# Loading w_q and w_o through ScalarE's DMA queue in a two-layer decode kernel

## The chip, the cores and the metric

The kernel runs on one core of a Trainium2 chip. The metric is device time in microseconds (us) of one execution. Before the change it is 644.1 us, the median of three runs (643.8 to 644.4).

## The reference, cut to what matters

Two identical layers, each of an attention block over cached keys and values and a SwiGLU block, for four sequences with one new token each. Both layers read the same caches and the same weights.

```python
B, Sq, D = 4, 1, 512
Hq, Hkv, Sk, Dh = 32, 8, 8192, 128

def _A_ref(x, k_cache, v_cache, wq, wo):
    q = transpose((x @ wq).reshape(B, Sq, Hq, Dh), 0, 2, 1, 3)
    k = jnp.repeat(k_cache, 4, axis=1)
    v = jnp.repeat(v_cache, 4, axis=1)
    scores = jnp.einsum("bhqd,bhkd->bhqk", q, k) * (Dh ** -0.5)
    o = jnp.einsum("bhqk,bhkd->bhqd", _softmax(scores), v)
    return transpose(o, 0, 2, 1, 3).reshape(B, Sq, Hq * Dh) @ wo

def _B_ref(x, w_gate, w_up, w_down):
    return (_silu(x @ w_gate) * (x @ w_up)) @ w_down

for layer in range(2):
    x = x + _A_ref(_layernorm(x), k_cache, v_cache, wq, wo)
    x = x + _B_ref(_layernorm(x), w_gate, w_up, w_down)
```

All tensors are bf16. The keys of one (sequence, key head) pair are 8192 x 128 elements, 2 MB (2,097,152 bytes), and its values as much. w_q is 512 x 4096 and w_o 4096 x 512, 4 MB each. Both layers together move some 273 MB from HBM to SBUF.

## The kernel before, in words

A *unit* is one (key head, sequence) pair, 32 of them in a layer, worked on in turn. For a unit the kernel loads all its keys into one of eight slots of the SBUF buffer `kv`, and all its values into another. VectorE transposes the keys in place, eight pieces of 128 x 512 (`turn`), TensorE makes the scores of each piece (`scores`), the softmax runs over ScalarE, TensorE and VectorE (`max_p`, `max_t`, `exps`, `turn_p`, `total`), and TensorE multiplies with the values (`values`). In every fourth unit the projection of a finished key head with w_o follows (`out_proj`), and the query of the next one with w_q (`qmul`). After the last unit of a layer comes the SwiGLU block (`ffn`). At the end of layer 0 the keys and values of three units stay in their slots for layer 1.

The loads. Every load of the kernel is issued by SyncE (`T.dma("sp", ...)`), in the order of the list `items`: keys and values as `work` gives them, K0 K1 V0 K2 V1 K3 V2 K4 V3 and so on, with the weights of the SwiGLU block at the end of each layer. `pump` goes through the list and issues a load as soon as its slot (`home`) is free, and stops at the first whose slot is not. K0 to K3 go to slots 0 to 3, V0 to V2 to slots 4 to 6; K4 needs slot 0 again, and V3 stands behind K4 in the list. `finished` frees a slot and calls `pump` again; a slot of keys is free when the last scores of the unit are done.

The two weights in question. w_q is kept in `wq_sb` as four tiles of 1 MB. Their four loads stand ahead of `pump`, with the load of x (4 KB) behind the first. w_o is kept in `wo_sb`, eight loads of 512 KB, in pairs put into `items` at places 3, 6, 9 and 12:

```python
for n, it in ((3, ("wo", 0)), (6, ("wo", 1)), (9, ("wo", 2)), (12, ("wo", 3))):
    items.insert(n, it)
```

`runs` views each source in HBM as rows of up to 32 KB, a multiple of 32 rows: 64 rows of 32 KB for the keys of a unit, 32 of 32 KB for a tile of w_q, 32 of 16 KB for a part of w_o. The load of a tile is written as an instruction on SyncE's queue by name (line 136 in the profile).

Who waits for them. The first `qmul` waits for the four tiles of w_q in turn (a semaphore for each). The cast in `out_proj` waits for all eight parts of w_o (one semaphore, `hold=[T.res["wo3"].w]`). In the order of VectorE's work, the transposes of K0 stand behind the first query's casts and placing, so they too come after w_q.

Instructions of TensorE, VectorE and ScalarE are first written on a tape and issued at the end of the build (`play`, `roll`), the regular units as a loop. A load that is issued with `T.dma` goes to its engine at once, ahead of whatever the tape holds. ScalarE's stream before the change starts with the load of its table of functions (line 313), and then its tape, which starts with the logarithm of the first normalization (`deviation`, behind the first block of scores).

Of the kernel before, what the change touches and what calls it, by code (L numbers as in the profile page):

```python
# [14 lines left out]
class _Rec:  # L15
    __slots__ = ("w", "r")

    def __init__(self):
        self.w = None
        self.r = {}  # L20
# [7 lines left out]

class _Sync:
    LATE = ("pe", "dve", "act")  # L30

    def __init__(self, nc, engines, prog_sems):
        self.nc = nc
# [5 lines left out]
        self.semval = {}  # L39
        self.tape = {n: [] for n in self.LATE}  # L40

# [72 lines left out]
    def op(self, engname, fn, reads=(), writes=(), sig=True, hold=()):  # L114
        left = self._open(engname, self._need(reads, writes)) + list(hold)
        if engname in self.LATE:
            name, args, kw = fn(_Call())
# [10 lines left out]
    def dma(self, engname, parts, sem, reads=(), writes=()):  # L128
        self._wait(engname, self._need(reads, writes))
        k = id(sem)  # L130
        for out_ap, in_ap in parts:
            e = self.eng[engname]
            if in_ap.shape[0] == out_ap.shape[0]:
                ins = e.dma_start(out_ap, in_ap)
            else:
                ins = e.add_instruction(mybir.InstDMACopy(  # L136
                    name=self.nc.get_next_instruction_name(), mode="Copy", queue="qSPDynamicHW",
                    ins=e.lower_ap_dma(in_ap), outs=e.lower_ap_dma(out_ap)))
            ins.then_inc(sem, 16)
            self.semval[k] = self.semval.get(k, 0) + 16  # L140
        self._record(engname, (sem, self.semval[k]), reads, writes)
# [5 lines left out]
def bass_interleave_layers__gqa_block_cached__swiglu_ffn__decode_kernel(  # L147
# [13 lines left out]
    _, G, S, Dh = A_k_cache.shape  # L161
# [3 lines left out]
    REP = Hq // G  # L165
    P = 128
    assert Dh == P and B * Hq == P and D % P == 0 and F % P == 0 and B == 4
    KT = D // P
# [15 lines left out]
    RUN = 1 << 15  # L184
# [8 lines left out]
    with ExitStack() as es:  # L193
# [27 lines left out]
        wq_sb = sb("wq_sb", [P, KT, HqDh], BF16)  # L221
# [3 lines left out]
        wo_sb = sb("wo_sb", [P, G, REP, D], BF16)  # L225
# [27 lines left out]
        n = 2 * FO * B  # L253
# [13 lines left out]
        def few(ap):  # L267
# [17 lines left out]
        sem_w = {n: [sem(f"sem_{n}{i}") for i in range(c)]  # L285
                 for n, c in (("wq", KT), ("wo", 1), ("wg", KT), ("wu", KT), ("wd", len(WD)))}
        sem_out = sem("sem_out")
        es.enter_context(nc.Block())
        T = _Sync(nc, engines, prog)
# [8 lines left out]
        for a in range(NA):  # L298
# [11 lines left out]
        T.op("dve", lambda e: e.tensor_reduce(own[:], acc[:, 0:QB].rearrange("p (a y) -> p y a", a=NA)[:, 0:NV, :],  # L310
                                              AX.X, ALU.max),
             reads=["acc"], writes=["own"])
        nc.scalar.preload_act_table_set("natural_log_exp_and_others")
        ones = onesf[:].to_broadcast([P, P])

# [22 lines left out]
        items = []  # L338
        for L in range(2):
            seq = [it for it in work(L) if it not in kept]  # L340
            for k, v in ((29, 27), (30, 28)):

                it = ("K", L, unit_order[L][k])
                seq.remove(it)
                seq.insert(seq.index(("V", L, unit_order[L][v])), it)
            items += seq + [("wg", L)] + [("wu",)] * (L == 0) + [("wd",)]
        for n, it in ((3, ("wo", 0)), (6, ("wo", 1)), (9, ("wo", 2)), (12, ("wo", 3))):
            items.insert(n, it)
        i, j = (items.index((k, 1, unit_order[1][2 * NRES + n])) for k, n in (("K", 1), ("V", 0)))
        items[i], items[j] = items[j], items[i]  # L350
        ends = [i for i, it in enumerate(items) if it[0] == "wd"]
# [17 lines left out]
                return 0 if i == NU - 1 else (7, 2, 3, 6)[i % CYCLE]  # L369
            return {NU - 3: 1, NU - 2: 4, NU - 1: 5}.get(i, (5, 0, 4, 1)[i % CYCLE])  # L370

        def runs(src):

            n = src.shape[0] * src.shape[1] * 2
            return src.rearrange("(r k) n -> r (k n)", r=32 * -(-n // (32 * RUN)))

        def load_weight(name, i=0):
            if name == "wq":
                T.dma("sp", [(wq_sb[:, i, :], runs(A_wq[i * P:(i + 1) * P, :]))], sem_w["wq"][i], writes=[f"wq{i}"])
            elif name == "wo":  # L380
                n = G // 4
                w = REP * Dh
                T.dma("sp", [(wo_sb[:, g, :, :].rearrange("p e n -> p (e n)"), runs(A_wo[g * w:(g + 1) * w, :]))
                             for g in range(i * n, (i + 1) * n)], sem_w["wo"][0], writes=[f"wo{i}"])
            elif name == "wg":
                for k in range(KT - i):
                    T.dma("sp", [(wg_sb[k], runs(B_w_gate[k * P:(k + 1) * P, :]))], sem_w["wg"][k],
                          writes=(places if k == 0 else []) + [f"wg{k}"])
            elif name == "wu":
                for k in range(KT):  # L390
                    T.dma("sp", [(wu_sb[k], runs(B_w_up[k * P:(k + 1) * P, :]))], sem_w["wu"][k], writes=[f"wu{k}"])
            else:
                for j, (a, b) in enumerate(WD):
                    T.dma("sp", [(wd_sb[:, a:b, :].rearrange("p e n -> p (e n)"), runs(B_w_down[a * P:b * P, :]))],
                          sem_w["wd"][j], writes=[f"wd{j}"])

        def pump():
            while issued[0] < len(items):
                n = issued[0]
                it = items[n]  # L400
                if it[0][0] == "w":
                    if it[0] == "wg":
                        if not {NKEEP, NKEEP + 1} <= free:
                            return
                        free.difference_update((NKEEP, NKEEP + 1))
                    load_weight(*it)
                    issued[0] += 1
                    continue

                s = home(it)  # L410
                if s not in free:
                    return
                free.remove(s)
                kind, L, u = it
                slot_of[it] = s
                g, b = unit_gb(u)
                cache = A_k_cache if kind == "K" else A_v_cache
                if it in split:
                    for i in range(len(pieces[L, u])):
                        part(it, s, i, i + 1, sem_l[i])  # L420
                elif (L, u) in pieces:
                    part(it, s, 0, len(pieces[L, u]), sem_s[s])
                else:
                    T.dma("sp", [(kv[:, s, :], runs(cache[b, g, :, :]))], sem_s[s], writes=[f"s{s}.{q}" for q in range(NB)])
                issued[0] += 1
# [126 lines left out]

        heads = {n: [] for n in T.LATE}
        blocks = []
# [352 lines left out]
        def roll(name):  # L907
# [43 lines left out]
                at = heads[name][n + CYCLE * turns]  # L951
            T.play(name, ops[at:])

        load_weight("wq", 0)
        T.dma("sp", [(xio, A_x.rearrange("b s d -> (b s) d"))], sem_x, writes=SCR)
        for i in range(1, KT):
            load_weight("wq", i)
        pump()
        xb = bank_bf(OUTB)
        for kt in range(KT):  # L960
# [4 lines left out]
        for L in range(2):  # L965
# [20 lines left out]
            for kind, _, u in todo:  # L986
# [9 lines left out]
             writes=[SCR[1]])  # L996
        T.wait_res("sp", reads=SCR)
        nc.sync.dma_start(out.rearrange("b s d -> (b s) d"), xio).then_inc(sem_out, 16)
        nc.sync.wait_ge(sem_out, 16)
        for n in T.LATE:  # L1000
            roll(n)
# [28 lines left out]
```

## Time and profile before

| | |
|---|---|
| median of three runs | 644.1 us (643.8 to 644.4) |
| the profiled execution: its own time | 644.4 us |
| its span, first to last instruction | 642.5 us |
| busy: PE, DVE, ACT, POOL | 80%, 70%, 19%, 3% |
| moved by DMA | 273.30 MB in 12215 packets, mean 425 GB/s |
| loads of keys and of values, whole | 56 and 56 of 2048 KB |
| loads of w_q, issue to landing | 4 of 1024 KB, median 8.5 us |
| loads of w_o, issue to landing | 8 of 512 KB, median 37.3 us (24.0 to 45.2) |

The profile is of one execution. PE is TensorE, PEld its weight loads, DVE VectorE, ACT ScalarE, POOL GpSimd, SP SyncE, SPq an instruction that issues a DMA. q1 is SyncE's DMA queue; q8 and q14 are queues over which the chip fetches its own instructions. Sixteen DMA engines serve all queues, and a load is spread over all sixteen. A row of the timeline has the start, the duration, the engine and line, the operation, its tiles and count, and in brackets the idle time before it with what ended it. A row of the DMA queues has the packets, their MB, and the time that they took as a share of sixteen engines' time in the stretch asked for; a packet belongs to the stretch in which it starts. A row of the stretches has, behind the stretch, its length, each engine's busy time and count, the clock granted to TensorE, the DMA share and GB/s.

### The profile page before, as it was taken

What the parts mean: (1) busy time and instruction counts of PE and PEld (TensorE: products, weight loads), DVE (VectorE), ACT (ScalarE), POOL (GpSimd) and SP (SyncE); (2) the same over time, 40 slices, a digit from 0 to 9 for tenths busy, and PEclk for the clock granted to TensorE, in tenths of its full rate; (3) what the DMA queues carried; (4) which work ended last, traced back from release to release, by engine and by line L of the source; (5) the groups of instructions that cost most, each with busy time, mean ns of one, the idle gap of its engine ahead of it and who ended that gap; (6) DMA issues with size and microseconds to landing.
All of it is one profiled execution on the core that took longest, in us unless ns stands there. A gap on an engine that the chain in (4) does not pass through costs nothing.

```text
span 642.5 us, 13057 instructions
## 1 busy us (share of the span) xinstructions
PE 514.2 (80%) x5064; PEld 332.7 (52%) x5087; DVE 450.9 (70%) x1108; ACT 122.1 (19%) x401; POOL 19.3 (3%) x73
## 2 busy tenths in 40 slices
PE   1757697887879788787888889898887769788788
PEld 1534454554546555455556655565554535555456
DVE  2646667677776867768764749987776776776783
ACT  0111211112212212212221422221221221221222
POOL 0000000000000000000000000000000000000000
PEclk9976779689896978999999989998889897987899
DMA  8999999999999999999999999999999999999996
GB/s 355 424 427 431 441 425 428 441 435 426 431 437 437 426 430 439 433 432 426 435 420 427 420 432 430 430 429 432 435 430 430 435 435 430 430 435 437 425 424 286
DMA packets 12215, 273.30 MB, mean 425 GB/s; under 512 B 2872, under 2 KB 2880, under 8 KB 3008
## 3 DMA queue, kind: packets, MB, share of 16 engines
q1 hardware_dynamic: 12192, 272.98, 99.1%
q8 instruction: 16, 0.26, 0.2%
q14 instruction: 7, 0.06, 0.0%
HBM read 272.96 MB, written 0.00 MB: 425 GB/s over the span
## 4 chain that ended last, share of the span: by engine, by line
DMA 61%; PE 22%; DVE 13%; issue 1%; SPq 1%; ACT 1%; DVEq 0%; POOL 0%; POOLq 0%
DMA kvf<-in_A_k_cache_dram 49%; PE ps L100 22%; DMA kvf<-in_A_v_cache_dram 9%; DVE kvf L118 8%; DMA kvf<-in_B_w_up_dram 3%; DVE acc L118 2%; SPq L136 1%; DVE one L118 1%; ACT pb L118 1%; DVE pT L118 1%; DVE m L118 1%; ACT acc L118 0%; POOL zq L502 0%; DVE oT L118 0%; ACT one L118 0%
## 5 line engine op out<-in xcount | busy, mean ns | idle before, releaser
L118 DVE STREAM_TRANSPOSE kvf<-kvf 128x512 f32<-128x512 f32 x488 | 322.6, 686 | 86.7 <-DMA kvf<-in_A_k_cache_dram 86.5
L100 PE MATMUL ps<-kvf,zq 128*128 128x256 bf16 x2048 | 316.7, 297 | 17.0 <-DVE kvf L118 12.6
L100 PEld LDWEIGHTS ps<-kvf,zq 128*128 128x128 bf16 x2048 | 196.9, 108 | 80.4 <-DVE kvf L118 29.6
L118 ACT ACTIVATE pb<-m 1x128 f32<-1x128 f32 x64 | 19.7, 308 | 431.6 <-DVE m L118 431.3
L100 PE MATMUL ps<-kvf,pT 128*16 128x512 bf16 x992 | 67.8, 395 | 10.4 <-DVE rl L118 6.3
L118 DVE SCALAR_TENSOR_TENSOR acc<-ps,own,acc 128x128 f32<-128x128 f32 x186 | 65.1, 350 | 5.4 <-ACT acc L118 0.7
L100 PE MATMUL ps<-identf,one 128*1 128x128 f32 x64 | 17.7, 277 | 49.1 <-DVE one L118 48.8
L100 PEld LDWEIGHTS ps<-identf,one 128*1 128x1 f32 x64 | 5.1, 79 | 77.8 <-DVE one L118 73.9
L100 PEld LDWEIGHTS ps<-kvf,pT 128*16 128x16 bf16 x992 | 19.4, 89 | 40.6 <-issue 22.3
L118 DVE TENSOR_REDUCE one<-ps 128x1 f32<-128x256 f32 x64 | 26.0, 407 | 16.9 <-PE ps L100 16.7
L118 ACT ACTIVATE pb<-ps,one,rstd 128x256 bf16<-128x256 f32 x64 | 36.1, 565 | 2.1
L502 POOL TENSOR_TENSOR zq<-scr,quad 128x64 bf16<-128x64 bf16 x62 | 18.2, 293 | 600.3 <-PE ps L100 473.4
L100 PE MATMUL ps<-head,acc 128*128 128x4 f32 x124 | 23.5, 260 | 15.6 <-DVE acc L118 15.6
L100 PEld LDWEIGHTS ps<-head,acc 128*128 128x128 f32 x124 | 21.2, 213 | 28.3 <-DVE acc L118 26.6
L100 PEld LDWEIGHTS ps<-one,pb 1*128 1x128 f32 x128 | 21.4, 208 | 26.9 <-ACT pb L118 22.6
L118 DVE RECIPROCAL rl<-ps 128x4 f32<-128x4 f32 x64 | 10.4, 162 | 34.2 <-PE ps L100 34.2
L100 PE MATMUL ps<-one,pb 1*128 1x1 f32 x128 | 26.8, 276 | 9.3 <-ACT pb L118 9.3
L118 DVE STREAM_TRANSPOSE pT<-pb 128x256 bf16<-128x256 bf16 x64 | 26.1, 408 | 4.6 <-ACT pb L118 4.5
L100 PE MATMUL ps<-wq_sb 128*128 128x512 bf16 (+1 forms) x84 | 26.2, 380 | 1.9 <-issue 1.1
L100 PE MATMUL ps<-xn,wq_sb 128*128 128x32 bf16 x284 | 19.6, 182 | 6.7 <-DMA wq_sb<-in_A_wq_dram 6.1
L100 PEld LDWEIGHTS ps<-o,wo_sb 128*128 (+1 forms) x256 | 20.0, 100 | 8.3 <-issue 4.5
L100 PE MATMUL ps<-o,wo_sb 128*128 128x32 bf16 x256 | 23.5, 181 | 0.8 <-DVE o L118 0.6
(72 smaller groups left out, 251.0 us busy)
## 6 DMA issues: line engine op xcount, KB each, us to landing
kvf<-in_A_k_cache_dram SPq DMA_DIRECT2D x56, 2048.0 KB, 28.9
kvf<-in_A_v_cache_dram SPq DMA_DIRECT2D x56, 2048.0 KB, 32.6
kvf<-in_A_k_cache_dram SPq DMA_DIRECT2D x7, 1024.0 KB, 7.7
kvf<-in_A_v_cache_dram SPq DMA_DIRECT2D x7, 1024.0 KB, 11.7
wq_sb<-in_A_wq_dram SPq DMA_DIRECT2D x4, 1024.0 KB, 8.5
wo_sb<-in_A_wo_dram SPq DMA_DIRECT2D x8, 512.0 KB, 37.3
kvf<-in_B_w_gate_dram SPq DMA_DIRECT2D x7, 448.0 KB, 18.0
kvf<-in_B_w_down_dram SPq DMA_DIRECT2D x12, 256.0 KB, 17.1
```

Of the source, the lines that this page charges most:

```text
L100: return e.matmul(out, lhsT=lhsT if at is None else lhsT(place(at)), rhs=rhs, **kw)
L118: self.tape[engname].append((repr((name, args, kw)), lambda e, _: getattr(e, name)(*args, **kw), left, sig, None))
L136: ins = e.add_instruction(mybir.InstDMACopy(name=self.nc.get_next_instruction_name(), mode="Copy", queue="qSPDynamicHW", ins=e.lower_ap_dm ...
L502: T.op(eng, lambda e: e.tensor_tensor(dst, q4, m4_, ALU.mult), reads=keys_ + ["quad"], writes=["zq"])
```

## The change

The loads of w_q and w_o are issued by ScalarE, on its own DMA queue, as the first instructions of its stream, ahead of the load of its table: four of w_q, then eight of w_o. SyncE's list holds the loads of x, the keys, the values and the weights of the SwiGLU block, which begin at once. Sizes, sources, destinations and semaphores of the loads are as before.

```diff
 class _Sync:
     LATE = ("pe", "dve", "act")
+    queue = {"sp": "qSPDynamicHW", "act": "qActDynamicHW"}
...
                 ins = e.add_instruction(mybir.InstDMACopy(
-                    name=self.nc.get_next_instruction_name(), mode="Copy", queue="qSPDynamicHW",
+                    name=self.nc.get_next_instruction_name(), mode="Copy", queue=self.queue[engname],
...
+        runs = lambda src: src.rearrange("(r k) n -> r (k n)", r=32 * -(-src.shape[0] * src.shape[1] * 2 // (32 * RUN)))
+        for i in range(KT):
+            T.dma("act", [(wq_sb[:, i, :], runs(A_wq[i * P:(i + 1) * P, :]))], sem_w["wq"][i], writes=[f"wq{i}"])
+        for g in range(G):
+            w = REP * Dh
+            T.dma("act", [(wo_sb[:, g, :, :].rearrange("p e n -> p (e n)"), runs(A_wo[g * w:(g + 1) * w, :]))], sem_w["wo"][0],
+                  writes=["wo3"])
         nc.scalar.preload_act_table_set("natural_log_exp_and_others")
...
-        for n, it in ((3, ("wo", 0)), (6, ("wo", 1)), (9, ("wo", 2)), (12, ("wo", 3))):
-            items.insert(n, it)
...
-            if name == "wq":
-                T.dma("sp", [(wq_sb[:, i, :], runs(A_wq[i * P:(i + 1) * P, :]))], sem_w["wq"][i], writes=[f"wq{i}"])
-            elif name == "wo":
...
-                T.dma("sp", [(wo_sb[:, g, :, :].rearrange("p e n -> p (e n)"), runs(A_wo[g * w:(g + 1) * w, :]))
-                             for g in range(i * n, (i + 1) * n)], sem_w["wo"][0], writes=[f"wo{i}"])
...
-        load_weight("wq", 0)
         T.dma("sp", [(xio, A_x.rearrange("b s d -> (b s) d"))], sem_x, writes=SCR)
-        for i in range(1, KT):
-            load_weight("wq", i)
         pump()
```

More of the change, by code (lines that the diff above doesn't have):

```diff
@@ L370, in home @@
             return {NU - 3: 1, NU - 2: 4, NU - 1: 5}.get(i, (5, 0, 4, 1)[i % CYCLE])
-        def runs(src):
-            n = src.shape[0] * src.shape[1] * 2
-            return src.rearrange("(r k) n -> r (k n)", r=32 * -(-n // (32 * RUN)))
         def load_weight(name, i=0):
-            if name == "wq":
-                T.dma("sp", [(wq_sb[:, i, :], runs(A_wq[i * P:(i + 1) * P, :]))], sem_w["wq"][i], writes=[f"wq{i}"])
-            elif name == "wo":
-                n = G // 4
-                w = REP * Dh
-                T.dma("sp", [(wo_sb[:, g, :, :].rearrange("p e n -> p (e n)"), runs(A_wo[g * w:(g + 1) * w, :]))
-                             for g in range(i * n, (i + 1) * n)], sem_w["wo"][0], writes=[f"wo{i}"])
-            elif name == "wg":
+            if name == "wg":
                 for k in range(KT - i):
```

## The prediction

> **What bounds the kernel now.** I read the page first, its slices of DMA use and its queues:
>
> ```profile
> span 642.5 us, 13057 instructions
> ...
> DMA  8999999999999999999999999999999999999996
> GB/s 355 424 427 431 441 425 428 441 435 426 431 437 437 426 430 439 433 432 426 435 420 427 420 432 430 430 429 432 435 430 430 435 435 430 430 435 437 425 424 286
> ...
> q1 hardware_dynamic: 12192, 272.98, 99.1%
> ```
>
> The reader is to see that no slice between the first and the last has idle DMA engines. PE is busy 80% and DVE 70%, so they are not the bound; the 99.1% of q1, SyncE's queue, is. Second, the busy time of stretches, for the rate with two digits more (the last two columns are the DMA share and GB/s):
>
> ```profile
> 2.50:6.00 3.50, 0.10 (x4) 0.11 (x4) 0.42 (x3) 0.00 (x0) 0.00 (x0) 1.00 0.89 357
> 6.00:11.00 5.00, 1.14 (x8) 0.78 (x7) 0.96 (x6) 0.00 (x0) 0.00 (x0) 1.00 1.02 406
> 11.00:16.00 5.00, 1.04 (x30) 0.74 (x30) 0.53 (x3) 0.00 (x0) 0.00 (x0) 1.00 0.99 426
> 96.00:320.00 224.00, 182.22 (x1680) 116.32 (x1686) 165.06 (x398) 41.78 (x143) 6.75 (x23) 0.89 1.00 432
> 365.00:600.00 235.00, 197.63 (x1871) 127.41 (x1875) 177.23 (x432) 46.19 (x156) 7.62 (x26) 0.92 1.00 432
> ```
>
> 432 GB/s is the plateau; 273.3 MB at that rate are 632.7 us of the span. What is left is some 3.5 us at the start (nothing moves before 2.1 us; the ramp to 16 us loses 3.5x75/432 + 5x26/432 + 5x6/432 = 1.0 us) and the tail. So the change, which moves the same bytes, counts only by DMA time that it wastes or saves. Third, the timeline of the start:
>
> ```profile
> 0.74 1.28 ACT L313 ACT_TABLE_LOAD   x1 [0.74 <-PEq L1015]
> 0.74 0.56 SPq L136 DMA_DIRECT2D wq_sb<-in_A_wq_dram  x1
> ...
> 14.36 0.53 PE L100 MATMUL ps<-xn,wq_sb 128*128 128x32 bf16 x13 [2.25 <-DMA wq_sb<-in_A_wq_dram]
> ...
> 19.17 6.72 DVE L118 STREAM_TRANSPOSE kvf<-kvf 128x512 f32<-128x512 f32 x11 [3.22 <-DMA kvf<-in_A_k_cache_dram]
> ...
> 21.23 0.26 ACT L118 ACTIVATE vs<-ps,one 128x4 f32<-128x4 f32 x1 [19.21 <-PE ps L100]
> ...
> 26.75 0.47 SPq L136 DMA_DIRECT2D kvf<-in_A_k_cache_dram  x1
> ...
> 36.92 0.71 DVE L118 STREAM_TRANSPOSE kvf<-kvf 128x512 f32<-128x512 f32 x1 [6.38 <-DMA kvf<-in_A_k_cache_dram]
> ```
>
> w_q is complete at 14.36, the first keys at 19.17, the first slot is refilled from 26.75, and at 36.92 compute has already been waiting 6.4 us for the third keys.
>
> Fourth, the DMA queues in stretches of 4 to 8 ns that each hold one packet's start, for what it costs an engine to serve a second queue. Share x 16 engines x stretch is the packet's time:
>
> ```profile
> q1 hardware_dynamic: 1, 0.03, 947.7%
> q1 hardware_dynamic: 1, 0.02, 636.5%
> q8 instruction: 1, 0.02, 753.1%
> q1 hardware_dynamic: 1, 0.03, 1345.3%
> q14 instruction: 1, 0.01, 386.2%
> q1 hardware_dynamic: 1, 0.03, 2263.8%
> ```
>
> Row 1 (at 32.57, 8 ns): an ordinary 32 KB packet, 9.477x0.128 = 1.213 us. Row 2 (40.01, 6 ns): an ordinary 16 KB one, 0.611. Row 3 (33.78, 8 ns): 16 KB of instructions on q8 between two q1 packets, 0.964, that is 0.353 over row 2. Row 4 (34.73, 8 ns): the q1 packet right behind it, 1.722, that is 0.509 over row 1. Row 5 (45.79, 5 ns): 8 KB on q14, 0.309, about in proportion to row 2. Row 6 (46.10, 5 ns): the q1 packet behind that, 1.811, 0.598 over. The pair at 368.5 and 369.5 gives 0.993 and 1.725. So q1, which is full all the time, loses about half a microsecond on an engine whenever another queue has had one packet there.
>
> **The change, part by part.** *SyncE loses 12 issues* (4 of w_q at 0.576 us, 8 of w_o at 0.596: 7.1 us). Keys are issued from about 1.3 instead of 3.73. Nothing is gained: the engines have a backlog either way, and the first packet comes 1.35 us after the first issue, at 0.74 on either queue.
>
> *ScalarE gains them ahead of the table load*: 7.1 + 1.28 us, done by about 9.1; 16.2 if each issue took twice as long beside SyncE's. Its first work is at 21.23, so the cover is 5 to 12 us and the cost nothing. Queued behind the issues on ScalarE are only the table load and that logarithm.
>
> *w_q now shares the engines with K0 and K1.* If both queues get alternate packets of 32 KB, w_q's 4.19 MB are in when 8.39 MB have moved: 8.39/0.432 + 3.5, plus the 1.1 us by which 14.36 lies behind the same sum for 4.19 MB, gives 24.0. Transposes start 1.6 us after w_q (15.95 against 14.36 in the trace: the projection, two casts, the placing), at 25.6 instead of 19.17; K4 is issued 7.6 us later (26.75 - 19.17), at 33.2 instead of 26.75. What covers this is the queue: 7 slots of 2.097 MB wait on SyncE's queue and 8.39 MB on ScalarE's, 23.07 MB, good to 23.07/0.432 + 3.5 = 56.9. The refill is 22 us early. Compute reaches K2 at 25.6 + 7.6 + 5.2 = 38.4 (5.2 is the step from the issue of K4 to that of K5), K2 lands at about 38, against 36.92 now; the delay is gone after two units. Once compute is behind it catches up: from 391.69 to 446.82, where it was behind, eight issues of keys lie 7.9 us apart, against 4.19/0.432 = 9.7 us of DMA per unit.
>
> *w_o* is in by (8.39 + 12.58)/0.432 + 3.5 = 52 instead of 74 (28.5 + 45.2 to landing); its first use is at 81.8. No gain, no cost. The order of all keys and values stays.
>
> *Two full queues on each engine.* This is the one unknown. Per engine, w_q is 8 packets of 32 KB and w_o 16 of 16 KB: 24 excursions from SyncE's queue, which holds 28 data packets at that time. The Trainium skill (DMA: Bandwidth & Descriptors, Queues, rings and completion order) has each engine go round the queues with work, a packet at a time, and rows 3 and 5 show single packets let in; it prices no switch. Bounds per excursion: nothing (or the ramp's 1.0 us gained in all) if two loaded queues overlap; 0.86 to 0.89 by the q8 pairs. The return to a loaded queue (0.47 to 0.6 in the rows) I count whole, 0.49; going in is 0.38 by q8 and nothing by q14, and I take half, 0.19. I take the switch as real because every such pair of the trace has it, though those queues are nearly empty ones, unlike ScalarE's. Sum: 24x0.68 = 16.3 us; ends 24x0.49 = 11.8 and 24x0.88 = 21.1. Since nothing before the tail has slack on the DMA side, all of it arrives at the end. It also moves w_q by 8x0.68 to 29.4 and K4 to 38.6, while the queue lasts longer too.
>
> Total: the profiled execution took 644.4 (span 642.5 and 1.9 around it), so 660.7; against the median of 644.1, 660.4.
>
> **Rivals.** *Overlap.* The loss in rows 4 and 6 belongs to instruction fetches, and two loaded queues feed an engine without a gap. Then only the order of 8.39 MB changes in a saturated stream and the time stays at 644.1, 643.1 at best if a second issuer mends the ramp. This ends on the other side, not slower; it decides if packets of 32 KB beside the other queue take about 1.21 us of an engine. For it: row 5 has no entry cost, and rows 1 and 2 take time in proportion to their bytes, so no latency shows within a queue. Against: rows 4 and 6. The Trainium skill (same page, Issuing engines are not separate DMA queues) says the same as this rival: all queues run on the same 16 engines and interleave, and a second issuer saves issue time alone; by that the sum is 644.1.
>
> *The edit does not act as two queues*: the engines serve SyncE's queue first. w_q then lands at (14.68 + 4.19)/0.432 + 3.5 + 1.1 = 48.3, K4 goes out at 57.5 and moves at 58.9, 2.0 us after the queue ran dry at 56.9; with a little more before the slots are refilled, 646 to 648. It decides only once w_q lands after 46.3. Served the other way round, ScalarE's first, w_q is at 14.4 and the time 644.1; this goes with the first rival. Single packets let in speak against both.
>
> **How the numbers follow.** Switch cost 0.45 (655.9 to 665.2, likeliest 660.4); overlap or weights first 0.38 (643.1 to 645.2); SyncE first, or overlap with a small price of each switch, 0.15 (645.5 to 652); 0.02 otherwise. A measurement here can tell about 0.2%, 1.3 us. Of the overlap case 0.05 may be faster by more than that, since the ramp holds only 1.0 us, and 0.33 within. Slower: 0.45 + 0.15 + 0.02. The range goes from the ramp's gain to the top of the switch case, 643.1 to 665.5; the likeliest case's own is 655.9 to 665.2.
>
> **What would show it.** Right: the slices of the first 70 us drop to about 300 to 350 GB/s while two queues are listed, packets of SyncE's queue in them take about 1.7 us, from 70 us on 432 returns, and all later issues of keys lie some 16 us later. Wrong: 425 or more in those slices (overlap), w_q landing after 46 with idle DMA near 57 (SyncE first), or a shift that arises later than 80 us, for which nothing here gives a reason.

## The result, and the profile after

The changed kernel takes 655.52 us (median of five runs, 655.04 to 656.14) against 643.92: the ratio is 1.018, interval 1.0165 to 1.0195. It is slower by 11.6 us, 1.8%, and clear of noise. That is the direction that was forecast and lies inside the range, 4.9 us below the forecast time; but it lies in the range of none of the cases from which the range was made (SyncE first ends at 652, the switch case begins at 655.9), and the cause is another one than the prediction named, as the profile and the experiments show.

The page of the kernel after (slices of 16.3 us, and the DMA queues; q10 is ScalarE's):

```profile
span 653.1 us, 13080 instructions
...
DMA  8998599999999999999999999999999999999997
GB/s 370 429 433 375 180 426 435 431 429 436 431 434 429 432 431 436 431 432 436 430 426 423 431 418 446 417 443 423 442 425 436 431 431 431 429 438 429 433 423 293
...
q1 hardware_dynamic: 11616, 264.59, 94.4%
q10 hardware_dynamic: 576, 8.39, 3.2%
```

The first three slices, in which both queues have loads, move no less than before (370, 429 and 433 GB/s against 355, 424 and 427). The hole is in the fourth and fifth, 49 to 82 us. The busy time of stretches, before first and then after, in the same columns as ahead (only the last two, DMA share and GB/s, matter here):

```profile
16.00:60.00 44.00, 29.09 (x217) 19.28 (x221) 25.23 (x53) 5.63 (x19) 0.88 (x3) 0.81 1.00 428
60.00:80.00 20.00, 13.10 (x93) 8.10 (x94) 12.90 (x31) 3.54 (x12) 0.59 (x2) 0.76 1.02 437
```

```profile
2.50:6.00 3.50, 0.65 (x3) 0.57 (x3) 1.29 (x9) 0.00 (x0) 0.00 (x0) 1.00 1.00 412
16.00:60.00 44.00, 9.46 (x81) 6.74 (x81) 11.39 (x22) 0.00 (x0) 0.29 (x1) 0.74 1.01 434
60.00:80.00 20.00, 7.73 (x58) 5.15 (x59) 4.93 (x12) 5.03 (x14) 0.29 (x1) 0.63 0.49 175
96.00:320.00 224.00, 192.46 (x1784) 123.45 (x1782) 175.21 (x422) 43.05 (x146) 7.31 (x25) 0.90 1.00 433
```

Up to 60 us nothing is lost; from 60 to 80 us 175 GB/s are moved instead of 437, 20 x 262 / 432 = 12.1 us of DMA time. In the first 60 us the two queues moved some 0.3 MB more than the one queue did (54 GB/s against 105 up to 2.5 us, 416 against 386 up to 11, 432 against 428 up to 60), 0.7 us. The difference, 11.4 us, is about the longer span (653.1 against 642.5, 10.6). After 80 us both run at the same rate.

The stretch from 16 to 60 us also shows ScalarE (the fourth pair of columns) with no work at all, where it had 5.63 us before. The timeline says why:

```profile
0.74 2.55 ACTq L137 DMA_DIRECT2D wq_sb<-in_A_wq_dram  x4
...
3.32 66.24 ACTq L137 DMA_DIRECT2D wo_sb<-in_A_wo_dram  x8
...
31.71 0.47 SPq L137 DMA_DIRECT2D kvf<-in_A_k_cache_dram  x1
...
32.22 0.60 SPq L137 DMA_DIRECT2D kvf<-in_A_v_cache_dram  x1
...
69.58 1.28 ACT L322 ACT_TABLE_LOAD   x1 [69.58 <-DMA wo_sb<-in_A_wo_dram]
...
75.66 0.47 SPq L137 DMA_DIRECT2D kvf<-in_A_k_cache_dram  x1
```

The eight issues of w_o spread over 66 us, the table load comes at 69.58, and between V3 (32.22) and K5 (75.66) SyncE issues nothing. The chain of waits up to 80 us has the links one by one (start, duration; the first also has the loads of w_q ahead of it in the queue):

```profile
3.32 23.25 DMA wo_sb<-in_A_wo_dram
26.58 8.66 DMA wo_sb<-in_A_wo_dram
35.26 8.38 DMA wo_sb<-in_A_wo_dram
43.66 8.55 DMA wo_sb<-in_A_wo_dram
52.23 9.55 DMA wo_sb<-in_A_wo_dram
61.80 3.71 DMA wo_sb<-in_A_wo_dram
65.53 3.52 DMA wo_sb<-in_A_wo_dram
69.08 0.48 ACTq L137
```

Each load of w_o is issued when the one before has landed. The reader can find the wait in the diff. The class `_Sync` keeps track of who last wrote and read each resource, by its name alone, and all eight calls of `T.dma` name the same resource, `writes=["wo3"]`. `dma` begins with `self._wait(engname, self._need(reads, writes))`, and `_need` adds the last writer of every resource that is written. So, from the second call on ScalarE waits for the semaphore of its own previous load, though the eight loads fill eight different parts of `wo_sb`. Before, each pair had a name of its own (`wo0` to `wo3`), and nothing waited.

How it gets from there to the DMA queue, by the waits of the first 100 us:

```profile
ACT L322 <- DMA wo_sb<-in_A_wo_dram: 69.6, 1, 69.6
...
PE ps L101 <- ACT pb L119: 37.4, 1, 37.4
DVE pT L119 <- ACT pb L119: 37.2, 1, 37.2
```

In TensorE's order the scores of K1 are mixed with the softmax of K0. TensorE stops for 37.4 us in the middle of K1, behind ScalarE, so K1's slot is not freed and K5 isn't issued; all later loads stand behind K5 in `items`. What was queued by then ran out at about 62 us: stretches of 4 us have 451 GB/s from 56 to 60, 279 from 60 to 64, 193 from 64 to 68, and 135 from 68 to 72, where before they have 414, 414, 463 and 430.

### The profile page after: what moved, and what is told of

It reads as the page before. It is cut to its first block, busy times and chain, and to the rows that moved or that the text cites. A ratio compares the mean times of both kernels' runs of the same rounds, so it can differ in the third digit from the quotient of the medians.

```text
span 653.1 us, 13080 instructions
## 1 busy us (share of the span) xinstructions
PE 513.0 (79%) x5087; PEld 332.8 (51%) x5087; DVE 449.6 (69%) x1108; ACT 121.9 (19%) x401; POOL 19.3 (3%) x73
## 3 DMA queue, kind: packets, MB, share of 16 engines
q10 hardware_dynamic: 576, 8.39, 3.2%
## 4 chain that ended last, share of the span: by engine, by line
DMA 53%; PE 23%; DVE 19%; issue 2%; SPq 1%; ACT 1%; ACTq 0%; DVEq 0%; POOL 0%; POOLq 0%
DMA kvf<-in_A_k_cache_dram 29%; PE ps L101 23%; DVE kvf L119 12%; DMA kvf<-in_A_v_cache_dram 11%; DMA wo_sb<-in_A_wo_dram 10%; DVE acc L119 4%; DMA kvf<-in_B_w_down_dram 3%; SPq L137 1%; DVE one L119 1%; DVE m L119 1%; DVE pT L119 1%; ACT pb L119 0%; ACTq L137 0%; DVEq L944 0%; DVE oT L119 0%
## 5 line engine op out<-in xcount | busy, mean ns | idle before, releaser
L101 PE MATMUL ps<-kvf,zq 128*128 128x256 bf16 x2048 | 312.4, 295 | 13.5 <-DVE kvf L119 6.6
L101 PE MATMUL ps<-xn,wq_sb 128*128 128x32 bf16 x284 | 23.0, 178 | 18.6 <-DMA wq_sb<-in_A_wq_dram 18.5
L101 PE MATMUL ps<-wq_sb 128*128 128x512 bf16 (+1 forms) x107 | 33.4, 397 | 0.0
L101 PEld LDWEIGHTS ps<-xn,wq_sb 128*128 (+1 forms) x284 | 18.2, 97 | 22.2 <-DMA wq_sb<-in_A_wq_dram 18.9
```

The costliest lines, as they stand in the source:

```text
L101: return e.matmul(out, lhsT=lhsT if at is None else lhsT(place(at)), rhs=rhs, **kw)
```

## The experiments

Theory H (ScalarE is held by the chain of waits) stood against Q (ScalarE's DMA queue accepts only about five loads, which the timeline alone would also allow, since five issues went out at once) and S (the price of a change of queue, the prediction's own term). All times are medians; ratios are against the kernel before, run on the same chip.

**The eight loads without the waits.**

```diff
-        for g in range(G):
-            w = REP * Dh
-            T.dma("act", [(wo_sb[:, g, :, :].rearrange("p e n -> p (e n)"), runs(A_wo[g * w:(g + 1) * w, :]))], sem_w["wo"][0],
-                  writes=["wo3"])
+        w = REP * Dh
+        T.dma("act", [(wo_sb[:, g, :, :].rearrange("p e n -> p (e n)"), runs(A_wo[g * w:(g + 1) * w, :])) for g in range(G)],
+              sem_w["wo"][0], writes=["wo3"])
```

> The changed kernel, but the eight loads of w_o are issued in one call, so that the tracker makes none of them wait for the one before it. Theory H (ScalarE is held: all eight loads are booked as writers of wo3, so each issue waits until the load before it has landed, and the softmax behind them starts only at 70 us): the eight issues follow each other in some 5 us, the table load comes at about 9 us, DMA does not run dry, time 643.0 to 644.5 us. Rival Q (ScalarE's DMA queue takes only about five loads at a time): the sixth issue still waits until some 25 us and the last until 60 to 70; time 650 to 656. Rival S (the prediction's term: engines lose time at each change of queue): the issues go out at once, but DMA moves 300 to 350 GB/s until 60 us and the time is 652 to 656.

Measured: 643.26 us, ratio 0.9992 (0.9983 to 1.0001). The same loads on the same queue in the same order, and the whole loss is gone. Its timeline and its stretches from 16 to 60 and 60 to 80 us:

```profile
3.34 5.55 ACTq L137 DMA_DIRECT2D wo_sb<-in_A_wo_dram  x8
...
8.92 1.28 ACT L321 ACT_TABLE_LOAD   x1 [8.92 <-issue]
...
37.04 0.47 SPq L137 DMA_DIRECT2D kvf<-in_A_k_cache_dram  x1
```

```profile
16.00:60.00 44.00, 27.70 (x232) 19.27 (x233) 25.35 (x56) 5.62 (x19) 0.88 (x3) 0.86 1.00 428
60.00:80.00 20.00, 14.94 (x124) 8.68 (x123) 13.84 (x34) 3.54 (x12) 0.58 (x2) 0.84 1.03 442
```

Twelve loads are accepted in 8.2 us, so Q falls; K5 goes out at 37.04 instead of 75.66. S falls too: here 24 packets per engine stand on ScalarE's queue while SyncE's is full, the DMA moves 428 GB/s from 16 to 60 us as in the kernel before, and nothing measurable is lost (the interval ends at 1.0001).

**Three waits instead of seven.**

```diff
-        for g in range(G):
+        for h in range(0, G, 2):
...
-            T.dma("act", [(wo_sb[:, g, :, :].rearrange("p e n -> p (e n)"), runs(A_wo[g * w:(g + 1) * w, :]))], sem_w["wo"][0],
+            T.dma("act", [(wo_sb[:, g, :, :].rearrange("p e n -> p (e n)"), runs(A_wo[g * w:(g + 1) * w, :])) for g in (h, h + 1)], sem_w["wo"][0],
```

> The changed kernel with w_o in four calls of two loads, so that ScalarE waits three times instead of seven. Theory H with a threshold: the first refill that hangs on the softmax is K5; it is issued 6.1 us after ScalarE is let go (69.58 to 75.66 in the changed kernel) and moves 1.35 us later, while the queued 27.3 MB last until about 66 us. So ScalarE may be let go up to 58.5 us at no cost, and each us beyond costs one. Four links: let go at about 50 us (30, 40, 50), no dry DMA, time 643.0 to 645. Rival Q and rival S: as for a_free, 650 or more.

Measured: 644.23 us, ratio 1.0016 (1.0007 to 1.0025). The links were longer than estimated, ScalarE was let go at 58.05 instead of 50, which is at the threshold, and 1.0 us over the free version is what is left:

```profile
58.05 1.28 ACT L322 ACT_TABLE_LOAD   x1 [58.05 <-issue]
...
64.62 0.47 SPq L137 DMA_DIRECT2D kvf<-in_A_k_cache_dram  x1
```

**ScalarE held with no chain**, behind the free version's loads. The added line waits for the first landing in slot 7 of `kv`, which is V3:

```diff
+        nc.scalar.wait_ge(sem_s[7], 16)
         nc.scalar.preload_act_table_set("natural_log_exp_and_others")
```

> As a_free (w_o in one call), but ScalarE waits ahead of its table load until V3 has landed, at about 66 us. Theory H: only the time at which ScalarE is let go counts, not how w_o was issued. Let go at 66: K5 is issued at 72, moves at 73.5, the queue is dry from 66, loss 7.5 us over a_free: 650 to 652. Rival Q or S: the wait adds nothing to what the queue already costs in a_free, the time equals that of a_free.

Measured: 654.07 us, ratio 1.016 (1.0145 to 1.0176). The loss is 10.8 us over the free version instead of 7.5. V3 landed at 68.04, later than the 66 expected, and K5 followed 6.57 us behind it instead of 6, which is 2.6 of the 3.3 us; the rest is not explained:

```profile
68.04 1.28 ACT L322 ACT_TABLE_LOAD   x1 [68.04 <-DMA kvf<-in_A_v_cache_dram]
...
74.61 0.47 SPq L137 DMA_DIRECT2D kvf<-in_A_k_cache_dram  x1
```

**ScalarE held with no second queue**: the same line in the kernel before.

> The kernel before (all loads on SyncE's queue), with ScalarE waiting ahead of its table load until V3 has landed, at about 64.5 us. Theory H: the loss needs no second queue. K5 issued at about 71, moving at 72, the queue dry from 66.6: some 5.5 us over before, 648.5 to 651. Rivals Q and S, in which the second queue costs the time: no change, 644, since the softmax has been early enough.

Measured: 651.97 us, ratio 1.0125 (1.011 to 1.0141), 1 us above the expected span, with ScalarE let go at 66.64 instead of 64.5:

```profile
66.64 1.28 ACT L314 ACT_TABLE_LOAD   x1 [66.64 <-DMA kvf<-in_A_v_cache_dram]
...
73.21 0.47 SPq L136 DMA_DIRECT2D kvf<-in_A_k_cache_dram  x1
```

The kernel with one DMA queue loses 8.5 us by the hold alone. Put together, with the time at which the table load starts in the profiled execution, and losses from the medians:

| kernel | ScalarE let go | loss | let go minus loss |
|---|---|---|---|
| three waits | 58.05 | 1.0 over free | 57.1 |
| held, one queue | 66.64 | 8.5 over before | 58.1 |
| held, free | 68.04 | 10.8 over free | 57.2 |
| the change | 69.58 | 12.3 over free | 57.3 |

The loss is the time past 57 to 58 us, about one for one, whatever holds ScalarE: by the chain of waits or by one wait, with two queues or with one. (The last row joins two sets of runs, in which the kernel before took 643.92 and 643.51. In the second row the profiled execution took 653.36, 1.4 above its median; by its own loss the last column is 56.8.) The threshold had been put at 58.5, from the step of 6.1 us between the table load and K5 (6.1 to 6.6 in these rows) and queued loads that last to 66 us.

**The parts that gain.** w_q alone on ScalarE's queue, as in the change but with w_o on SyncE's as before; and, as another kernel, x loaded first on SyncE's queue with all else as before. The edit of the second:

```diff
-        load_weight("wq", 0)
         T.dma("sp", [(xio, A_x.rearrange("b s d -> (b s) d"))], sem_x, writes=SCR)
-        for i in range(1, KT):
+        for i in range(KT):
             load_weight("wq", i)
```

> One part of the change alone: the four loads of w_q on ScalarE's queue, w_o on SyncE's as before. Theory H: nothing waits for a load ahead of the table load, the softmax is in time, 643.0 to 644.5. Rival S: eight packets per engine beside the other queue, 4 to 6 us slower, 648 to 650. Rival Q: four loads are still accepted, 644.

> The kernel before with one difference: x is loaded ahead of all four tiles of w_q instead of behind the first. It asks where the 0.6 us come from that the changed kernel gains on the ramp (window 2.5 to 11 us). If the small load of x between the large ones disturbs them, the ramp is as in the changed kernel and the time is 643.3, 0.6 us below before; if it needs a second issuer, the ramp and the time stay as before, 643.9.

Measured: 643.13 and 643.53 us, both ratios 0.9994 (0.9985 to 1.0003). S would have cost the first one 4 to 6 us. For the second the question stays open: its rate from 0 to 16 us is 361 GB/s, as in the changed kernel and in w_q alone, against 355 before, so some of the 0.6 us on the ramp may go with the place of x; but these are single profiles, and none of the free version, w_q alone and x first can be told from before in time. No version found here is measurably faster than the kernel before.

## Why the prediction was right and where it was wrong

**What bounds the kernel** held: the loss is DMA time that was not used, and it appears whole at the end.

**SyncE's lost issues, w_q and the refill of K4** came about as worked out: w_q complete at 22.98 (24.0 without a price of switches, 29.4 with it), K4 issued at 31.71 (33.2 and 38.6). So these two times, too, fit two queues that take turns at no price. Neither costs anything, as the free version and w_q alone show.

**ScalarE's issues** is the step that failed. "Done by about 9.1" counted twelve durations and no wait; in the kernel without the waits the table load is over at 10.2, so the durations were right. The text looked at what is queued behind the issues, and asked how long they take if each were twice as slow, but not what each issue waits for; the resource name in the diff tells it. In the changed kernel the step ends at 70.9. With it fell the time of w_o: its last load was issued at 69.08, where all of it was to be in by 52.

**"The delay is gone after two units"** failed with it: it followed the keys, and not the softmax that stands between the scores in TensorE's order. ScalarE had a cover of its own, up to 57 us by the table of the experiments, and the change went 12 us past it.

**Two full queues on each engine**, 16.3 us in the sum, is nothing that these runs can measure. The free version is the test, with all twelve loads on ScalarE's queue by 8.9 us: 0.9992 (0.9983 to 1.0001). Single packets in the profile of after, in stretches of 8 ns as in the prediction (at 30.72 and 31.33 us; share x 16 x 0.008):

```profile
q10 hardware_dynamic: 1, 0.02, 477.3%
q1 hardware_dynamic: 1, 0.03, 947.7%
```

16 KB on q10 take 0.611 us and the 32 KB on q1 that start as they end take 1.213, the same as rows 2 and 1 of the prediction, with no change of queue. So the rival "overlap" described the queues rightly, and the Trainium skill's rule beside it (DMA: Bandwidth & Descriptors, Issuing engines are not separate DMA queues) agrees with the traces: over 16 to 60 us 428 GB/s in the free version and 428 before (434 in the changed kernel, where ScalarE's queue had one load of w_o at a time from 26.58 us on). The price on instruction fetches is in the profile of after too (0.988 us for 16 KB on q8 at 38.07), but it was carried over from those queues to a loaded one without a row that joined them.

The two errors made up for each other: a term of 16.3 us that isn't there, and a wait of 12 us that was left out. That the time fell in the range is luck, and no support for the reasons given. Of the signatures that were listed, the slices did not fall to 300 to 350 while two queues are listed; they stood at 429 and 433, and fell to 375 and 180 only when SyncE's queue had run dry; and the packet of SyncE's queue above took 1.213 us and not 1.7. That contradicts the switch cost by the prediction's own test.

**SyncE's queue first** fell with w_q at 22.98. Its mechanism, a refill that comes after the queue has run dry, is the one that decided, but behind ScalarE's wait and at K5, not behind w_q at K4.

## What to carry to other kernels

Where loads move into the stream of an engine that computes, count for each issue what it waits for, before its duration: a tracker like this one, which books parts of one buffer under one name, makes every load wait for the one before, and here the engine's other work stood behind all of them. Work out how long the queued transfers last and which refill hangs on that engine; up to that point a delay cost nothing here, beyond it every microsecond counted, even though the DMA was busy 99% of the time. A price seen on one kind of queue is no likeliest value for another kind until a row joins the two.

## What the runs showed of the hardware that was not expected

Two loaded queues shared the sixteen engines with no loss that could be measured (packets of 0.611 and 1.213 us, 428 GB/s over 16 to 60 us in the free version, a ratio of 0.9992). Beside a loaded queue, a 16 KB packet of instructions took 0.353 us longer than 16 KB of data, and the packet behind it 0.509 longer than usual (rows 3 and 4 of the prediction). Why the two differ was not tried. ScalarE issued twelve loads, 8.39 MB, in 8.2 us without stalling (free version).
